# A searched order of products for attention beside a gated layer: another order, its constants, and an earlier spread of one unit's inverses

## The chip, the core and the metric

The kernel runs on one core of a Trainium2 chip. The core has a matrix engine (TensorE, PE in the profile; its weight loads, which overlap the products, are PEld), VectorE (DVE), ScalarE (ACT), GpSimd (POOL) and a queue engine (SyncE, SP), which issues all the DMAs here. Each engine runs its own instructions in the order in which they were written and waits at semaphores for the others. The metric is the device time of one execution in microseconds (us).

## The reference

With x of 2048 rows and 512 columns, float32:

```python
q = (x @ wq).reshape(B, S, H, Dh).transpose(0, 2, 1, 3)      # 32 heads of 16
k, v = x @ wk, x @ wv                                        # one key and value head for all
p = softmax(einsum("bhqd,bkd->bhqk", q, k) * Dh ** -0.5)
a = einsum("bhqk,bkd->bhqd", p, v) ... @ wo                  # heads back to rows, 512 x 512
b = (sigmoid(x @ w_gate) * (x @ w_up)) @ w_down              # 1792 wide
g = sigmoid((x * gate_w).sum(-1, keepdims=True))
out = g * a + (1 - g) * b
```

## The kernel before, in words

The 2048 rows are cut into four blocks of 512. A *unit* is four heads of one block: 32 units (NU), numbered by block and then by group of heads. A unit has four kinds of work.

- *Maximum* (`maximum`, L1141 and L1143): PE multiplies queries with keys, and VectorE reduces each bank of 128 x 512 scores to maxima, which are sent through memory into two spare rows of the queries (`send_max`, `place_max`).
- *Scores* (`scores`, L1150 and L1152): PE multiplies keys with queries, now less the maximum, and ScalarE takes the exponential out of the bank.
- *Values* (`pv`, L1008): PE multiplies the exponentials with the values and a column of ones, in float32, for one of 16 chunks of keys. One call leaves eight matrix records in the trace. Runs of chunks are summed in a bank; at the end of a run ScalarE copies the bank out (`finish`, L1015) and POOL adds it to the unit's sum (`add_sums`, L1022).
- *Division*: the sum is stored (`store`, sd and od), its denominators are loaded in another shape (`sums`, rc), VectorE inverts them (`invert`, L1045), they are stored (`send_inverse`, rd, L1049), loaded back spread over the rows of a head (`spread`, bc, L1055), and POOL multiplies and splits the result into a high and a low part (`divide`, L1063, then L755 and L756: tile o). Two units share one o. The last unit but one (30, NU - 2) has an o of its own: its `spread` issues two loads of bc and two of vd (L1055, L1057), and its `divide` follows alone. Unit 31 is finished at the very end by other code.

Beside this run the projections (`keys`, `query`, `turn`: early, letter G) and the *filling* products (`fill`, L1115): gate, up and down of the second layer, and the output projection of the attention. Jobs of kind "a" project a block's units with wo; for the last block, two jobs "a" do all but the last of four parts, two jobs "e" project unit 30 (they read o), and unit 31's part comes at the end (L1196).

PE's rows are used in two halves of 64. A *pair step* issues one product in each half, of maximum, scores or filling. A filling job fills two banks and changes them over between its halves: when a half has done its first part, an empty instruction on SP (`nc.sync.nop()`, L1119, made in `fill`) waits for that product, and the other half's second part waits for it. The empty instruction stands in SP's own order among the DMAs.

The order of PE is a string, ORDER. V is one chunk of values, G a projection, a dot a pause of the planner's clock of 25 units that issues nothing, and any other letter a hexadecimal digit: its two parts, over 4 and modulo 4, are what each half does (1 maximum, 2 scores, 3 filling, 0 nothing). Before the kernel is written out, `plan()` walks through the string with a clock of its own, in units of a hundredth of a pair step. For each step it puts down the work that follows (banks to reduce, copies, sums, DMAs) at the place at which, by its constants, that work may begin; these places set the orders of the other engines. LATE, RED, EXP, COPY and so on are those constants; FREE and FREE_A are what passes until a bank is free again; IN and OUT are the changes between V or G and pair steps, VALUES one chunk. `event` handles the chain of the division, `may` and `run` the tasks of POOL, and `issue_f` reckons when a turn-over is seen.

In the planner's division chain each link is put down at the first step after its due time. `store` adds 470 to SP's clock and is due to land before `sums`; then come `invert`, `send_inverse`, `spread` and `divide`:

```python
elif what == "send_inverse":
    self.after(self.send(1, 8) + SAFE, "spread", *args)
elif what == "spread":
    u = args[0]
    at = self.issue(250, 128)
    if u % 2 or u == NU - 2:
        self.task(2, at + 2 * SAFE, "divide", u)
```

`send` and `issue` give the time at which the planner takes the data to have landed. No link of the chain changes its own instruction by being put down elsewhere; on the chip each instruction still waits for the data that it reads.

Of the kernel before, what the change touches and what calls it, by code (L numbers as in the profile page):

```python
# [26 lines left out]
NU = NB * NG  # L27
# [10 lines left out]

LATE, LATE_A, FREE, FREE_A = 190, 200, 65, 60


RED, GATED, SUM, ENDS, INVERSE, LOWER = 260, 258, 285, 115, 70, 285

MAX_SPLIT, SQUARE, SEND_SQUARE, PLACE = 180, 75, 220, 320
EXP, COPY, SCALED = 208, 210, 247
TAIL, TAIL_A = 38, 52

SEEN = 10  # L50


IN, OUT, VALUES = 52, 106, 371

CAST, TWO, CAST_W, TWO_W = 265, 556, 450, 1030

# [1 line left out]
ISSUE, SMALL, TEN_KB, LAST, SAFE, SURE = 185, 750, 20, 300, 300, 150  # L58
# [64 lines left out]
class State:  # L123
# [170 lines left out]
    def event(self, what, args):  # L294
        self.acts.append((what, *args))
        if what == "load_x":
            self.x_loaded[args[0]] = self.send(KC, 1024)
        elif what == "store_q":
            at = self.send(2, 512)
            self.q_ready[tuple(args)] = at  # L300
            self.ba_release(("query", *args), at)
        elif what == "send_max":
            self.after(self.issue(SEND_SQUARE, 16) + SAFE, "place_max", *args)
        elif what == "max_square":
            self.after(self.on("dve", self.now, SQUARE) + TAIL, "send_max", *args)
# [360 lines left out]


ORDER = (
    "GGGGGGG555G55G555G55........5GG55G555GG555GG77777Gffdfdffffddddddfffffffff7775.5..GG555GG555G55G9efef7ee7edf6f9f"
    "fb777b7bfefedeedfbd9fbfb75VVV5edeeedff6f9fbb7ef7b7b7bbdfdebfd9fb7bffddd5VV566VVVV977b7bbff9f6fef6defedeedef7ede7"  # L670
    "fbf9bf6bffb5VV555VVVdedef97bf6f6fee7fbdb7b7bbfddefb7edb7ff7ddd5VVVV7b7bb7fedbdbdbe7fedededeef7b7fb7be7dbffddd5VV"
    "VVV67bbb77ffedaf7dbfededeeddbfb7b7fb7ef6efdfd5VV665VVVV7b7bb7bfdedbbd7efedededee7f7bf9fbf67bfedef5VVVVV7b7b7bb7f"
    "bdbdedefedededeef7b7fb7edb7bffddd5VV659VV97b77bbffedaf77efededeede7fb7fef6f9e7fbdbf5VVV555VVV7b7bb7fbdedbdedbfe7"
    "eededef7e7f9f6fedbff7b79V659VV566VVdedeb7f9fe7bdef9e7fb7bb77fbbdbfe6fdfbdfddd5VVV566VV56aV97fefbdbdbf6fb7bfdeded"
    "ee7fb7b7edbe7fedff755VVVVVdededeedef7be7b7fb7b7bb7bfdedfbde7bf9fbdef5VV656VV959VV7b7b79fbfbde7edbfededeede7fb7f6"
    "f9fee7b7ffd9V659VV656VVVded6effb79fef9f6fe7b7bb7bdfdbfbdbf9e7fedef5VVVVV7b9bb77ff9feed7bedfededeef77bbf7b7eded7f"
    "7ddVVVV6b7fedf9f6fbdee7fedb7b7b7ef9fdef6fbedfbdb7dVVV659VV6a5V7b7bbdfededeedb7f6fafbV595VVV7b7bbdfededeed7bfe7bb"
    "dVV9b7b7f7ef6febdfbfdedededbfb76fee7e7f9fe77dbVVVVVVdedeedede7f6fb7bbf7b7b7bbdff9fb7eeded7bffd5VV655VVVdede6fe7f"
    "b7ef9f6f9fb7b7bbdfedfe7edbf9fb7fdaVVVVV7b7bb7b7bfdedebdfedededeef7e77bfbdb7bfedef5VV655VVV7b97b7bffbdbdef9fedede"
    "dedbfb7ef76fef6fb7ef5V9a6VV665VV959VV6dedefe7fedb7bb7defb7bb7bfdbdfedb7be7effee6V959VV956VV956VV7b7afddbf9f6fbed"  # L680
    "fb7ededeef7b7f9f6fbf6fedf75VV59aV692aVV569VV56effedefbdaf7f6bfdb7b7bbdfdbbfd6fef7f7ddd5VVVV7b7bdbedfe7ef6dbfb7ed"
    "ededbf7bb7f6fedebfdfb5VVVVV7b7b79bffbdafdf6fededeedef7e7fb7e7eedff7b5bV95aVVVVV977bfbdef9fb7e7ebdfedeedef7b77bf9"
    "fef6f9ff5eV595VVVVV7b7b7bbdf9fafde7edfedeede7ff6ef7edb7bfefb7aV995VVV565VV7b7b7bbdfeedfedb7fededee7ef7edef97efb7"
    "bbd7bVVV599VVV7b7bb77bbdfbededfedededeef77eef7edbb7fefb75VVVV9edff6edf6fef97bdbfb7b7bbfd6fdefedef7df7775VVV959VV"
    "97b7fbdefbdeb7f9f6fededeef7b7f9faf7b7deff5dVVVVV7b7edbdbf6f9fb7bfededeedef7e7f6f6fef9fb7fb9VVVV969VV6b7bfde7fed6"
    "fede7efbb77bbdfedfedbdb7eeffb75VV596VV596VV997ffbf6f9fbb7dbefdededee7f6ff6f9f7efbff79aVV955VVVV7b7b7b9ff9fbe7edf"
    "edededee7ff6fb76fedefbfb76VV5a9VVVde5eefb7f9fee7dbfbf7ba77fedfedef9bf7bdff755VVVVVdeded6effb7bf9f6fe7b7bb7bfd9ff"
    "ed6fbdeff75dbVVVV65aV6deedffb7b7b7bdbffdde5VV696Vdede6fbf7b7b7bdefbdfd6VVV9b7fde7bfbdbdbb7fedededeef76ffb7bfa7fd"
    "ff5d5VVVVV7b5bbffedb7ee7bdf6fededeedf7bf6faf7f9fff7aaVVV995VVVdee6fdf6fe7bb7fedfb7b7bbdfbd9fef9f6fe7ffd56VVVV6ed"
    "ededff6fb7be7fbdb7b7bbfdedfb79febdf6fef5VV665VV995VV6deedf7bfb7eedf6fbdb77bb7efdeedfedbf9bf7fb5V695VV956VV95aVV6"  # L690
    "7bff9dbf6fef6eddefb7bb7bdfbd7bf6fedefbfedaV695VV695VVVV7b7b7bf9fbdef6.dbdefedeedef7b7ef6fdef6ff7b5a..7V599VV5aaV"
    "V96aVV6eddfef6f6f9fe7bbfdb77bb7efedfed9fbf9b7fdf5VV569VVVV7b7bb7fededeb7f9fe7edededbf7bfe7bb7edbfdfd5VVVV677bbfd"
    "ef6f9feb7bfdededee7fb7ef79fe7bfffd55VVV659VV7b97bfbfded6fbbdf6feeddee7f7bf6fafdf6fbdf5bVVVVV6deef7dbf6fafd7bedfb"
    "7bb7bfdedf9feb7f6bdfef5VV956VVV97bb7b7ffbdedbe7fededeede7fb7fede7bbdf7f7d5VVVVV97fb7bdefb79fbe7efdededee7fb7dbfe"
    "7bdbf6fefaV955VVVVV6dedefe7f6fb7ebdef7b7bb7bdf9ffbdbde7ebfdfd6V695VVVV7b7b7bbdf9fbedf6fedededee7f7ef6f6febdfb7bf"
    "6V959VVVVV6deedef7fe7bedb7dbfb7bb7bdfedefd6fbdbfff575VVV9a6VV696V6ddeeff9f6f9fe7bfbdb7bb7bdff97bfedb7efedef5VV66"
    "9VV559VVV7b7b7bf9fbdeed7efe7ededeef7b7fedef6f9fb7bf9VV569VV6deeeddffb7bf6deb7fb7bb7bdf9ffe7bdeedff7d57VVVVV977bb"
    "7bffbdbedf9fedeeddee7f6ff6f6fbb7efdf76VVV995VVV5b7b7bfefed9fe7bf9fedededef6ff6fb7bfbdeb77dVVV955VVV7b97fbfededed"
    "efefbb7afdfffe7b7b7bf6fedfe5VVVV6dedefe7fe7bbddbfe7b7bb7bdfbdf6fedbe7bdff5dVV659VVV7b7bb7bdf9febd7efededeede7f7e"
    "bf7bde7bf7fde9VVV5a6VV59aV7b7b7b7bbfdbdeedfedededeef7e7fe7e7bf9fbdf75VVVVVV5eedef7efe79febdfb7b7b7bbfd9fbdfb7bf6"  # L700
    "defeddVV655VVV7b7bb7bdfbde7edbdefededee7fe7fe7b7bbddeff76V9a9VV665VV596VV5bbfdeefde76fbdef9f7bb7bbfddbfb7be7f9ee"
    "fedeV659VV695VV56aVV6ddeef7efedb7ebdb7fb7bb77efedfedbdbb7fedf5bV956VV5aaVV96aVVV97bff9e7f6fbf9f97efededeef7b7f9f"
    "6fb7ff7ddd5VVVV7b7bb77bfedbf9defedededeef7b7fe7b7edeef7bf5VV596VV956VV95effef6fedbedf6fb7b7b7bbfdedfbde7ebdbff7d"
    "5VVVV65aV6ddefbf9fe7ef6f9fbdb7b7bbfd7befdbde7efbdd7dVVVVV67bb7bfdf9fbf6edef7ededeef7b7f9faf7dbfe7efbb777VVVVVV9f"
    "dbbdfbe6fdfedededeef76fbf6fdb7efb7f95VV955VVV7b7b97bffedef6dbf9fededeef77e7bf6fef9bbffd5VVVVV7b7b7bb7fedafdedfbd"
    "ededeef7b7fe7e7ef9f9ff76V595VVVVded6fbf6fede7bf97efb7bb7bdff9fb7edeb7dffdd6VV659VVV5e7bfebdfe7edeb7fedbb7b7bbfdf"
    "f9b7fe7fdeded6VV966VVVV7b7bb7dbf9fbdeffedededee7fe7ef6edfefb7b7b79VV959VVVV7b97fbe7f9fbdee7fe7edeedef7dbfaf9f7ef"
    "7ff759VVV966VV5bb7feedfbde7edefe7b7bb7bdff9defedb7e7fd7f6VVV999VVV7b7bb7fedbdef9f6fe7ededee7ffbde7b7befdbb5fdV59"
# [548 lines left out]
```

## Time and profile before

| what | value |
|---|---|
| median of three runs | 1583.95 us (1583.82 to 1584.93) |
| time of the profiled execution | 1582.52 us |
| its span, first to last instruction | 1580.7 us |
| busy: PE, PEld, DVE, ACT, POOL | 1567.2, 1009.0, 1338.9, 1232.2, 803.8 us |
| granted clock of PE, mean | 0.998 |
| DMA | 103.43 MB, mean 65 GB/s |

The largest groups are the reduction of the maxima on VectorE (2048 times, 1253.7 us busy), the exponentials on ScalarE (2048 times, 1040.2 us), and on PE the products of scores, maxima and values. Busy times of PE overlap: two halves run side by side, so the groups of PE add to more than its span. A matrix record's duration includes the time through the array; the distance from start to start tells the pace. The profiled execution's own time is 1.8 us longer than its span, and 1.4 us shorter than the median of the runs.

### The profile page before, as it was taken

The page shows a single profiled execution, that of the slowest core. Times are in us where ns is not written, and L with a number is a line of the kernel's source. Part 1 is how long each engine was busy: PE and PEld are TensorE (multiplying, and loading weights), DVE is VectorE, ACT ScalarE, POOL GpSimd, SP SyncE. Part 2 cuts the span into 40 slices and gives each one's busy share as a digit, 9 for nine tenths or more (in the row PEclk, how much of TensorE's full clock was granted, in tenths as well). Part 3 has the DMA queues.
Part 4 walks back from the last instruction along what each step waited for, and adds up shares of the span by engine and source line. Part 5 has one row for each costly group of instructions (what it writes and reads, how often), then busy time and mean ns, then how long its engine had stood idle before and what let it go on. Part 6 is the DMA issues. An engine that isn't in the chain of part 4 may idle for free.

```text
span 1580.7 us, 33642 instructions
## 1 busy us (share of the span) xinstructions
PE 1567.2 (99%) x12910; PEld 1009.0 (64%) x12910; DVE 1338.9 (85%) x2277; ACT 1232.2 (78%) x2429; POOL 803.8 (51%) x727
## 2 busy tenths in 40 slices
PE   9999999999999999999999999999999999999997
PEld 7766666666666666666666666667675666656653
DVE  6899899988898888889798888888889888988841
ACT  4277878788788787878788777878878887878895
POOL 4353472655574164367475346275547517357351
PEclk9999999999999999999999999999999999999999
DMA  7421120222122121122122212021213202111011
GB/s 245 169 88 51 35 86 16 66 62 83 43 83 66 36 79 53 35 76 71 45 83 63 64 49 78 18 67 60 77 46 92 65 23 87 46 40 59 18 53 40
DMA packets 63076, 103.43 MB, mean 65 GB/s; under 512 B 24530, under 2 KB 24786, under 8 KB 62916
## 3 DMA queue, kind: packets, MB, share of 16 engines
q1 hardware_dynamic: 62916, 101.29, 20.5%
q8 instruction: 101, 1.65, 0.4%
q14 instruction: 59, 0.48, 0.1%
HBM read 79.51 MB, written 21.75 MB: 64 GB/s over the span
## 4 chain that ended last, share of the span: by engine, by line
PE 96%; DVE 1%; DMA 1%; SPq 1%; ACT 0%; issue 0%; POOL 0%; DVEq 0%; ACTq 0%; POOLq 0%
PE bank L1115 32%; PE bank L1008 29%; PE bank L1141 17%; PE bank L1150 16%; PE bank L853 2%; DVE mx L1143 1%; DMA vd<-od 0%; DMA wqr<-wq 0%; SPq L968 0%; DVE q L948 0%; DMA qs<-qd 0%; ACT x L780 0%; PE bank L1196 0%; DVE x L786 0%; SPq L765 0%
## 5 line engine op out<-in xcount | busy, mean ns | idle before, releaser
L1143 DVE TENSOR_REDUCE mx<-bank 128x1 f32<-128x512 f32 x2048 | 1253.7, 680 | 168.7 <-PE bank L1141 104.0
L1152 ACT ACTIVATE p<-bank 128x512 f32<-128x512 f32 x2048 | 1040.2, 664 | 10.9 <-PE bank L1150 7.7
L1150 PE MATMUL bank<-qs,ks 64*128 64x512 f32 x2048 | 723.7, 399 | 0.0
L1141 PE MATMUL bank<-ks,qs 64*128 64x512 f32 x2048 | 684.2, 404 | 0.5 <-DMA qs<-qd 0.5
L1008 PE MATMUL bank<-p,v_aug 128*32 128x512 f32 x4096 | 480.6, 597 | 0.0
L1141 PEld LDWEIGHTS bank<-ks,qs 64*128 64x128 f32 x2048 | 339.8, 184 | 138.7 <-issue 56.5
L1150 PEld LDWEIGHTS bank<-qs,ks 64*128 64x128 f32 x2048 | 359.6, 184 | 91.3 <-ACT p L1152 27.8
L1015 ACT COPY ou<-bank 128x512 f32<-128x512 f32 x205 | 125.0, 610 | 272.3 <-PE bank L1008 124.1
L1022 POOL TENSOR_TENSOR ou<-ou,ou 128x512 f32<-128x512 f32 x174 | 224.3, 1289 | 170.2 <-ACT ou L1015 167.7
L1115 PE MATMUL bank<-wd,hl 64*128 64x512 f32 x1344 | 272.7, 391 | 0.0
L1115 PE MATMUL bank<-x,wu 64*128 64x512 f32 x1344 | 271.3, 390 | 0.6 <-SPq L1119 0.4
L1008 PEld LDWEIGHTS bank<-p,v_aug 128*32 128x32 f32 x4096 | 113.1, 109 | 248.4 <-issue 220.5
L1115 PE MATMUL bank<-x,wg 64*128 64x512 f32 x1344 | 271.2, 391 | 0.0
L1115 PEld LDWEIGHTS bank<-wd,hl 64*128 64x128 f32 x1344 | 199.8, 184 | 20.6 <-issue 2.5
L1115 PEld LDWEIGHTS bank<-x,wg 64*128 64x128 f32 x1344 | 200.8, 184 | 17.5 <-issue 1.2
L1115 PEld LDWEIGHTS bank<-x,wu 64*128 64x128 f32 x1344 | 201.1, 184 | 17.0 <-issue 2.5
L1094 POOL TENSOR_TENSOR ba<-ba,pa_d 128x512 f32<-128x512 f32 x35 | 44.5, 1283 | 93.2 <-ACT pa_d L1091 93.1
L829 POOL CAST wg<-rg 128x1024 fp32r<-128x1024 f32 x27 | 28.0, 1039 | 123.8 <-PE bank L1115 63.9
L829 POOL CAST wu<-ru 128x1024 fp32r<-128x1024 f32 x27 | 28.1, 1040 | 95.8 <-PE bank L1115 93.2
L756 POOL TENSOR_TENSOR wd<-rd,wd 128x512 fp32r<-128x512 f32 x56 | 72.3, 1292 | 4.5
L756 POOL TENSOR_TENSOR hl<-h,hl 128x512 fp32r<-128x512 f32 x56 | 72.0, 1286 | 4.5
L1115 PE MATMUL bank<-wa,o 64*128 64x512 f32 x360 | 70.4, 391 | 0.0
(80 smaller groups left out, 747.2 us busy)
## 6 DMA issues: line engine op xcount, KB each, us to landing
rg<-wg SPq DMA_DIRECT2D x28, 512.0 KB
ru<-wu SPq DMA_DIRECT2D x28, 512.0 KB
rd<-wd SPq DMA_DIRECT2D x28, 512.0 KB
qs<-qd SPq DMA_DIRECT2D x192, 64.0 KB
qd<-q SPq DMA_DIRECT2D x32, 256.0 KB
od<-ou SPq DMA_DIRECT2D x31, 256.0 KB
xf<-x_in SPq DMA_DIRECT2D x16, 256.0 KB
vd<-od SPq DMA_DIRECT2D x32, 128.0 KB
```

Source lines behind the costliest of these rows:

```text
L756: lo.tensor_tensor(hl[:, 1, :], raw, f32(hl[:, 0, :]), op=ALU.subtract)
L829: nc.gpsimd.tensor_copy(WS[item][:, 0, :], raw)
L853: nc.tensor.matmul(ps, w[:, p, part(kc)], X[b, kc][:, q, :], start=i == 0, stop=i == 3 * KC - 1)
L1008: nc.tensor.matmul(ps[32 * j:32 * j + 32, :], v_aug[:, c, :], PT.pop((u, c, j)), start=start, stop=stop)
L1015: nc.scalar.copy(to, ps)
L1022: nc.gpsimd.tensor_tensor(SUMS[u], SUMS[u], PARTS_OF[u].pop(0), op=ALU.add)
L1094: nc.gpsimd.tensor_tensor(BA[b, t], BA[b, t], PA[b, t].pop(0), op=ALU.add)
L1115: ins = nc.tensor.matmul(banks[i], l, r, start=start, stop=stop)
L1141: nc.tensor.matmul(banks[i], qs_t[u % 3][r, pr, part(qt)], ks[r, kb * 512:(kb + 1) * 512], start=True, stop=True)
L1143: nc.vector.tensor_reduce(MX[u][:, pr, h, qt, kb:kb + 1], banks[i], axis=AX.X, op=ALU.max)
L1150: nc.tensor.matmul(banks[i], ks[r, part(c)], qs_t[u % 3][r, pr, :], start=True, stop=True)
L1152: nc.scalar.activation(p, banks[i], AF.Exp, scale=0.25)
```

## The change

Four things change; the functions that issue instructions stay as they are.

- The string ORDER is another one throughout. Both strings issue the same products: 512 V, 24 G, 2048 maxima, 2048 scores and 4404 filling products, in 4251 pair steps before and 4252 after, with 14 dots before and 19 after, 209 runs of full steps (V or G) before and 208 after.
- Constants of the planner are set anew.
- For unit 30, `spread` is due as soon as SP has issued `send_inverse`, and no longer when its data are taken to have landed.
- For unit 30, `divide` is due 1000 units later after the spread than before.

```diff
-LATE, LATE_A, FREE, FREE_A = 190, 200, 65, 60
+LATE, LATE_A, FREE, FREE_A = 186, 190, 62, 62
...
+SPREAD_TWICE = 1000
-EXP, COPY, SCALED = 208, 210, 247
+EXP, COPY, SCALED = 209, 211, 250
...
-IN, OUT, VALUES = 52, 106, 371
+IN, OUT, VALUES = 52, 109, 373
...
         elif what == "send_inverse":
-            self.after(self.send(1, 8) + SAFE, "spread", *args)
+            at = self.send(1, 8) + SAFE
+            self.after(self.sp if args[0] == NU - 2 else at, "spread", *args)
         elif what == "spread":
             u = args[0]
             at = self.issue(250, 128)
             if u % 2 or u == NU - 2:
-                self.task(2, at + 2 * SAFE, "divide", u)
+                self.task(2, at + 2 * SAFE + (u == NU - 2) * SPREAD_TWICE, "divide", u)
...
 ORDER = (
-    "GGGGGGG555G55G555G55........5GG55G555GG555GG77777Gffdfdffffddddddfffffffff7775.5..GG555GG555G55G9efef7ee7edf6f9f"
+    "GGGGGGG555G55G555G55....5...G55GG555GGG555G5dddGf5fff7ffdf7f77..77fffffffff7ddd5GG555GG555GG7.5bfefefbdbfbdb7fed"
...
-    "VVV67bbb77ffedaf7dbfededeeddbfb7b7fb7ef6efdfd5VV665VVVV7b7bb7bfdedbbd7efedededee7f7bf9fbf67bfedef5VVVVV7b7b7bb7f"
...
-    "6VVVV7b7b7b7bfedeedf6dbfededeedff6fbd6fbe7bffb7aV9aaVV596VV956VVVd6eeffdb7bb7b7fed9ffe9VVV7b7bfedbdeededfefb7bb6"
-    "VVV7b7b7b7bfbdededbfedededee7fb7f6f6fedeefbb77V959VVVVde5eedeffb7b7ef6f9fb7b7bbfdf9fbdb7edbfedfe6V6aaVVaaaVVVaaa"
-    "VVVbbbffffefeafeaVVeffefeeffbbbbaVVaaaVVaaaVVabfffffafafbVVeeeeefffffebbbbVbffafbbVaaaVVeeea8VVVV"
...
+    "59VVVdedeedf6f6faf7dbfb7b7bb7bfddbdbfe7ebfde7afeV969V596VV655VVVdedefb7e7b7b7bfedbefadVV969V9b7b7ffedededef6fbfb"
+    "a7V65aV956VVVdedeeddeedfbb77fbb7b7.7b7bfbdbbdfedee7fbdeebVVVVV677bfbf9fbd6fbdefefde6defbf7bbfbffeffeeaa.VVaaaVVV"
+    "aaaVVVeeeffffebfbbbbbbffffffeee.aVVVaaaVVaaaVVbbbffebfffeeeceeeffffffbbbaVVaaaVVaaaVVabbbVVeeeeff3.a2VVV"
 )
```

More of the change, by code (lines that the diff above doesn't have):

```diff
@@ L668 @@
 ORDER = (
-    "GGGGGGG555G55G555G55........5GG55G555GG555GG77777Gffdfdffffddddddfffffffff7775.5..GG555GG555G55G9efef7ee7edf6f9f"
-    "fb777b7bfefedeedfbd9fbfb75VVV5edeeedff6f9fbb7ef7b7b7bbdfdebfd9fb7bffddd5VV566VVVV977b7bbff9f6fef6defedeedef7ede7"
-    "fbf9bf6bffb5VV555VVVdedef97bf6f6fee7fbdb7b7bbfddefb7edb7ff7ddd5VVVV7b7bb7fedbdbdbe7fedededeef7b7fb7be7dbffddd5VV"
-    "VVV67bbb77ffedaf7dbfededeeddbfb7b7fb7ef6efdfd5VV665VVVV7b7bb7bfdedbbd7efedededee7f7bf9fbf67bfedef5VVVVV7b7b7bb7f"
-    "bdbdedefedededeef7b7fb7edb7bffddd5VV659VV97b77bbffedaf77efededeede7fb7fef6f9e7fbdbf5VVV555VVV7b7bb7fbdedbdedbfe7"
@@ L674 @@
[L674 to L708, printed above, removed]
@@ L709 @@
-    "6VVVV7b7b7b7bfedeedf6dbfededeedff6fbd6fbe7bffb7aV9aaVV596VV956VVVd6eeffdb7bb7b7fed9ffe9VVV7b7bfedbdeededfefb7bb6"
-    "VVV7b7b7b7bfbdededbfedededee7fb7f6f6fedeefbb77V959VVVVde5eedeffb7b7ef6f9fb7b7bbfdf9fbdb7edbfedfe6V6aaVVaaaVVVaaa"
-    "VVVbbbffffefeafeaVVeffefeeffbbbbaVVaaaVVaaaVVabfffffafafbVVeeeeefffffebbbbVbffafbbVaaaVVeeea8VVVV"
+    "GGGGGGG555G55G555G55....5...G55GG555GGG555G5dddGf5fff7ffdf7f77..77fffffffff7ddd5GG555GG555GG7.5bfefefbdbfbdb7fed"
+    "edee7fe7ed6fedbfb7bf775VVVdedededefb7b7bf9f6fb7b7bbdfdbfb7bdef7dfddd5VVV659VV977bbf7ef6fbb7edfedededee7f7b7bf9fe"
@@ new lines @@
+    "7bfeedf5VVV6a6VVVVded9fb7fef6f6fedfb7b7bb7bfd9fbde7ef9fffdd55VVV699V977bbf7ef6fbb7defedededee7ff6fb7ede7ef7f775V"
+    "VVVV9dededeffb7bf97edbfb7b7bbdfbdb7fbde7ffdddd5VVVV7b7b7e7bf6fafdf6edfedeeddffa7fb7f6f9f6fff55VVVVVd6defe7ef6fed"
+    "bbdfb7b7bb7bdfbd7efbfe6fdff5d5VVVV6a5V5b7bbff9f9fe7bdbfedededee7f7ebf79fb7befedf9VV655VVVV67befd7ef9feed7eef7bb7"
+    "b7bdfdbfedbb7fe6dffd5VVVVVdedededefb7eb77efb7b7b7bbdff9fedb7bf6ffded5VV659VVV7b7bb7b7fbdededefe7deeedef7f6f9fbde"
+    "f7ff7755VVVVdedeeddefb76fb7efb77bbb7bfdededfedbdbfb7bf5VV659VVVV7b7bb7bfdedbdedbfbdededee7f7bfb76fe7bffded5VV565"
@@ new lines @@
+    "VVVdededeef7e7eb7bdfb7b7b7bbdfdbfbb7bffededed6VV669V5a6V955VVVdedeedef7b7ee77efb7bb7b7bdfbdf9fbdbdeff57ddVV65aV6"
+    "56VVdededefe76f9feb7fb7b7b7bbdfdbf9fbed7efedaf7VVV5a5VV669V5a6Vd9fef6feb77bb7f9fdfdd5VVV7b7bbfdededeedfb7bef57VV"
+    "6deeedf7f9fee7bdbf7b7b7bbdff9fe79fbfe6fdd7dVVVVV6b7efdf6fed6fbedef7b7b7bbfddeefd6fbdbfb7dd7VVVVV7b7bb7f9fbd9fef6"
+    "fedededee7ff6efde7bf9ff7b79V955VVV65aV95aV5eef7bbdfb79fb7bedfedeeddbf7bb7fb7ef6effed6VV659VVVV6b7b7fdbfbd9fbdbef"
+    "dedeede7fb7fe7eb77edeff75VV95aV5a5VVV7b7bdbdef9f6feb7f9fedededfee7ef7e7b7efbfbb9V696V595VVVV699V97b7bff9fe7ef6db"
@@ new lines @@
+    "7efedeede7ff6defedb7bfb7bd7V969V5aaVV695VVVV7b7b7bbfd9fafdf6fedeeddee7ff6fbdef6f9fb7bfdddddVVVVV6defb7f6fb76ffb7"
+    "bb7bdf6fbdeb7f9fbdefdd6VVVV677bbfdbf9fb7ef6edfedeede7f7eefd6fbf7fd7b75VV995VVV97b7fedbf9fbf6dbfe7ededeef7f6bdf6f"
+    "efe7b7f79VVVVV9deeddfefe7b7bdbfe7b7b7bbfdedef79fbe7efdbf5VV965VVVV97bb7b7ffbdef9f6fededeedef77ef9fe7ebd7bff79V65"
+    "aV956VV959VV977bfe7bf9febdb7fedededeef77ebf79fb7bdefef5VVVVV977b7bbffbdef6f9defeddeee7ff6fb7bdbf6f9ffd5VVVVV7b7b"
+    "7bf9fedbe7f6defededeef7b7fb7bdeedfff575VVVVV97b7fbedfbdbf67ef9fededeef77ebdfe7bdfbf6fb5VV699V659VVV7b7bf9e7fedbf"
@@ new lines @@
+    "9fe5bfedede.e7f6ffb7e7bedfb7df5..6VVV59aVVV5bb7bfdbfe7bdebdf6fededee7ff6fbd6f7deff7bbaVV9aaVVVV6b7fdedefbdef6f6f"
+    "9fb7b7bbdfdbbfdb7ede7efef9VV555VVV7b7b7b7bfed9fbedefdedeeddbf7b7bf6fbf6ffddd5VV655VVV6b7bf7defbde7bdbfe7edeededf"
+    "7bfe76fe7bdbff57VVVVVdedef6fb7b7b7bf9fefadeV9a6VVVdedefe7b7b7b7bfedbdf5dVV6deefd7efe7bf9edfb7b7b7bbdfbdfbdb7eed7"
+    "eff5dVVVVV7b7b7b7bbdfedebdefdededee7ff6fe7b7bf9fedf57VV956VVVde6eedf7fe7ef97bbdfb7bb7bdfedbf7edbedf7ff55VV696VVV"
+    "6dedfbdefe7bf97bfedbbb777eff9feedfb7edefbb9V655VVVVV6b7fdbbdfe7ebdf9fe79fe4..edbfb7e7edbdfef6fb7f99VV956VV569VV5"
@@ new lines @@
+    "befe7f9fb7b7eedfb7eeededf7fedbe7ef79fbfbb5VV9a5V6a5V695VV56aVVdedededee7feb77bfb7b7bb7bdfbdefd9fbb7ffde6dV956VVV"
+    "696VVV6fdeedf6fede7bfbf7b7bb7bdf9fbdbf6fbdedff65dVV566VVVd6defbdbfb7bf6f9fb7deeedef7f6f9f9fbe7fff575VVVVVdede7bf"
+    "e7edbdb7ef9f7b7b7bfbf9f9feed7efe7fd5VVVVde6deef7feb7bdfe7fb7b7bbdedfbd9fe7efb7bdd7eVV6aaVVVVVdededefe7b7bf97ef6f"
+    "bbb77bffdbdbdee7fbdefeb6V955VVV97bb77bffbdedbed7efedeedef7e7f9f6fbf6fff755VVV955VVVdededee7fbf6dbfb7fb7b7bbddef9"
+    "fb7bbde7fafdddVVVV67b7b7bffedb7edbedfededeef77bb7f9fbf6ffded5VV665VVVV6dedfe7efede7b7ebf7b7b7bbdfdebfd9fbf9fe7fd"
@@ new lines @@
+    "5VV665VVVVdedef6fb7edbede7fb7bb77bbdfdbf9fbf97efefeeaVV596VV596VV5edefedbf6fee77bf9fb77bb7bff9edfe7ebdffbed5VV65"
+    "5VVVdedede6ffe7eb7dbfb7b7b7bbfddbfbdb7bdeefde7dV956VVVVV6edef7def6fafd7efb7b7bb7bdff9f9fedbf6f6fef5VV956VVV5edef"
+    "efedb7bf9e7f6fb7bbb7fdfedbf9b7fedffd55VVVVV6dedef7bfe76fedbfe7b7b7bbdfbdbdf9fe7efe79fdVVVVV7b7bf9fededede7bfee77"
+    "7VVVdedeef7b7b7b7bfedbdef5VV9def7edbf6fef6f9fe7b7bb7bfdbdfbd6fbf9fed6fdVV696V699V565VVVd6defb7efbdef6f6f9fb7bb77"
+    "bff9efd9fe7eefff59VVV5a6VVVdede6edffb7ef97efb7b7b7bbdfdbfede7bdefaf7f5V95aVVVV6dfebdf6fe79fef6ef7b7b7bbdff9dbfbd"
@@ new lines @@
+    "bdee7fef5VV655VVVVdedede7bf6fee7bdbf7b7bb7bfdedbfd9fefe7af7f5V969V699V565VVV6deedf7bfb79fbf9bf7edeeddfb7bbf76fbf"
+    "6effedaV6a5V955VVVVV5edeedfbfe7af7f9f6fb7b7bbdfedf9fb7bf6ffded6V699V56aV569VVVV97fef6f9fedef6f6fbdb7b7bbfdf9fede"
+    "7bfe6fdf57VVVV5eedeedffb76fedbfb7b7b7bbdfbdeef5fbfedaff75VVVVVdedededee7f6fb7bfb7b7bb7bfdf9bfd6fbdbffdde6V655VVV"
+    "V966V5eedeedffb7ef6f9fb7b7bb7bfdedfbdbf9b7fed6fdVVV655VVV79fee7dbf6fede7ef9fb7b7bbfdbd7efbdbf6fefed5VV659VVV6dfe"
+    "f9f6f6fedebdfb7b7b7bbdfede7f9fef6dbffb5VVVVVdedeede7fb7ef67ebf7b7bb7bdfedfbdbdbf9f6ffe5VVVVV6deedf7ef9f6fef9fb7b"
@@ new lines @@
+    "7bb7bfdbdbdfb7ef7dfd5edVV656VVV5edefb7efede7bdefb7b7bb7bfdedf6fbdedebf7f75VV9aaVVVV97bbb7fdf6f9fbedfe7edeedef7e7"
+    "bf79fef6efd7bbVVVV9a9VV977bbfbdfe76febdfbdededeef7e77ef9fbb7bffed5VV655VVVV6daff7defede7bdb7efb7b7bbdff9defb7ef9"
+    "fe7fd6V6a5V555VVVVdedeedfb7b7bede7fe7bbb77bffd9fbdeb7feffed65VVVVVdededeedef7e7bb7fb7b7b7bbdfdedefbdef6ff7775VV9"
+    "59VVVdedeedf6f6faf7dbfb7b7bb7bfddbdbfe7ebfde7afeV969V596VV655VVVdedefb7e7b7b7bfedbefadVV969V9b7b7ffedededef6fbfb"
+    "a7V65aV956VVVdedeeddeedfbb77fbb7b7.7b7bfbdbbdfedee7fbdeebVVVVV677bfbf9fbd6fbdefefde6defbf7bbfbffeffeeaa.VVaaaVVV"
@@ L712 @@
+    "aaaVVVeeeffffebfbbbbbbffffffeee.aVVVaaaVVaaaVVbbbffebfffeeceeeffffffbbbaVVaaaVVaaaVVabbbVVeeeeff3.a2VVV"
 )
```

## The prediction

> **What bounds the kernel now.** I read the page first, then the busy time by stretches, the chain of waits at the end, and the issues of the DMA queue there. The page's first line and the chain:
>
> ```profile
> span 1580.7 us, 33642 instructions
> ...
> PE 1567.2 (99%) x12910; PEld 1009.0 (64%) x12910; DVE 1338.9 (85%) x2277; ACT 1232.2 (78%) x2429; POOL 803.8 (51%) x727
> ...
> PE 96%; DVE 1%; DMA 1%; SPq 1%; ACT 0%; issue 0%; POOL 0%; DVEq 0%; ACTq 0%; POOLq 0%
> ```
>
> TensorE (PE) is busy for all but 13.5 us of a span of 1580.7. The stretches say where those 13.5 us are (start:end, length, then busy time of each engine, granted clock, DMA):
>
> ```profile
> 5.00:100.00 95.00, 93.50 (x519) 69.25 (x520) 79.73 (x142) 40.29 (x73) 31.12 (x24) 1.00 0.53 181
> 100.00:1545.00 1445.00, 1444.43 (x12185) 924.91 (x12183) 1248.87 (x2117) 1170.26 (x2315) 764.79 (x691) 1.00 0.19 58
> ```
>
> From 100 to 1545 us PE lacks 0.57 us of work in all; from 5 to 100 us it lacks 1.50 us. So a new order can win nothing in the middle: PE has the same products to do, and only their count, the changes between kinds, and stalls can move the time. The stall worth having is in the last 30 us. The same view there:
>
> ```profile
> 1552.80:1555.90 3.10, 1.50 (x11) 0.34 (x9) 0.75 (x1) 2.43 (x5) 0.21 (x1) 1.00 0.19 69
> 1555.90:1559.30 3.40, 1.49 (x6) 0.77 (x8) 0.00 (x0) 0.00 (x0) 2.94 (x3) 0.50 0.00 0
> 1559.30:1562.70 3.40, 3.40 (x17) 1.43 (x17) 2.16 (x3) 2.06 (x4) 0.00 (x0) 0.50 0.00 0
> ...
> 1569.50:1572.90 3.40, 2.40 (x19) 0.86 (x14) 0.90 (x4) 0.86 (x4) 0.00 (x0) 1.00 0.00 0
> 1572.90:1576.40 3.50, 2.15 (x33) 0.56 (x33) 1.94 (x3) 1.09 (x3) 1.26 (x1) 1.00 0.13 48
> ```
>
> PE runs dry after 1554, and then its clock is granted at 0.50 up to 1562.7. The chain there (start, length, what):
>
> ```profile
> 1549.36 6.18 DMA vd<-od
> ...
> 1555.69 1.27 POOL vd L1063
> ...
> 1557.71 1.28 POOL o L756
> ...
> 1559.04 0.79 PE bank L1115
> 1559.83 0.43 PE bank L1150 x2
> ...
> 1561.53 1.60 PE bank L1008 x8
> 1563.13 0.88 PE bank L1150 x4
> ```
>
> PE waits for o of unit 30, made by POOL's divide of the last unit but one, which waits for the last of four loads. The first step with a product on o starts at 1553.81, and the third of them (it reads the low part) would have stood two pair steps later, at 1554.27; it ran at 1559.04: 4.77 us late. At half clock a step then takes 0.43 us.
>
> **The prices.** From the chain, a value step (8 records) and a pair step:
>
> ```profile
> 1296.60 0.66 PE bank L1141 x2
> ...
> 1307.65 0.55 PE bank L1008
> ```
>
> ```profile
> 1503.56 3.57 PE bank L1008 x32
> ...
> 1531.69 1.85 PE bank L1008 x16
> ...
> 1538.86 0.89 PE bank L1150 x6
> ```
>
> Forty-seven pair steps lie between the first two rows: 11.05 us. Three take 0.89. So a pair costs (11.05 - 0.89) / 44 = 0.231 us, and each stretch of pairs 0.20 more. Two values take 1.85 and four 3.57, so a value costs 0.86 and a run of values 0.13 more; a change of kind and back is 0.33.
>
> **The change, part by part.** *The order.* Counting the letters of both strings: V 512 and 512, G 24 and 24; pair steps 4251 and 4252; runs of full steps 209 and 208 (196 with values in each); dots 14 and 19; steps with one empty half 2 and 4, already in the pair count. That is +0.23 for the pair, -0.33 for the run: -0.1. A dot issues nothing, it moves the planner's clock by 25 units (0.06 us at 0.231 us per 100 units): between 0 and 5 x 0.06 = 0.3; I take 0, since all dots of before lie in stretches that lack next to nothing.
>
> *Early stretch.* Other pair steps stand between the projections. At most the 1.50 us are won; as much may be lost. I take 0 and keep +-1.5 for the range.
>
> *The constants.* They do not change what PE does in which order; they change when the planner believes a bank or a result to be there, so the order was allowed to stand closer to its producers. The path over VectorE (LATE + RED + TAIL + FREE) goes from 553 to 546 units, that over ScalarE (LATE_A + EXP + TAIL_A + FREE_A) from 520 to 513: 7 units or 16 ns less room. Where does PE stand at the limit? The weight loads' waits from 100 to 1500 us (total, times, longest) say it:
>
> ```profile
> PEld bank L1141 <- ACT p L1152: 30.4, 55, 0.8
> PEld bank L1150 <- ACT p L1152: 23.0, 61, 0.8
> ...
> PEld bank L1008 <- ACT p L1152: 8.6, 26, 0.6
> ...
> PEld bank L1008 <- DVE mx L1143: 6.6, 22, 0.4
> PEld bank L1141 <- DVE mx L1143: 5.2, 7, 0.8
> ```
>
> 171 places, most of them ordinary changes of kind. Sixteen ns at each is 2.7 us; nothing at each is 0 (and no gain is to be had, since PE lacks 0.57 us here). I take 0.4, near the lower end, because the middle hides its producers today almost wholly. SCALED may turn some sums made by ScalarE and POOL into sums on VectorE or back; both engines lie beside PE (85% and 78%): nothing, and where a queue is full, it shows as the stalls just priced.
>
> *The spread of unit 30.* The DMA queue (SP) at the end, with the unit before for comparison:
>
> ```profile
> 1503.02 0.31 SPq L1049 DMA_DIRECT2D rd<-rc  x1
> 1504.43 0.56 SPq L1055 DMA_DIRECT2D bc<-rd  x1
> ...
> 1535.95 0.56 SPq L1030 DMA_DIRECT2D sd<-ou  x1
> ...
> 1540.24 0.32 SPq L1049 DMA_DIRECT2D rd<-rc  x1
> 1547.60 0.57 SPq L1055 DMA_DIRECT2D bc<-rd  x1
> ...
> 1549.36 0.51 SPq L1057 DMA_DIRECT2D vd<-od  x1
> ```
>
> ```profile
> SPq L1119 <- PE bank L1115: 13.4, 3, 6.9
> ```
>
> The inverses are stored at 1540.24, and 1.41 us later (as for unit 29) they could be read: 1541.65. The four loads start at 1547.60. The second fence (the DMA queue's own waits from 1530 to 1560) has the reason: line 1119 is the empty instruction by which SP tells one half of PE that the other half's bank is turned over. It stands in SP's order ahead of the spread, and waits for a product that ends at 1547.4 (chain, below). That is 5.95 us lost.
>
> ```profile
> 1547.39 0.05 PE bank L1115
> ...
> 1564.02 1.85 PE bank L1008 x16
> ```
>
> ```profile
> 1553.81 0.49 PE L1150 MATMUL bank<-qs,ks 64*128 64x512 f32 x1
> ```
>
> After the change the four DMAs (two bc, two vd) stand right behind rd. They wait for rd's landing, with nothing of use behind them on SP until the output; on POOL nothing follows the divide before the last addition. SPREAD_TWICE only has the planner place the divide 1000 units (2.3 us) later. So far the wait would vanish. But the order around it is new. In the new tail, from the end F of unit 30's last value (before: 1531.69 + 1.85 = 1533.54), come V aaaVV aaaVV, then 27 pair steps, then VV aaaVV aaaVV a, and the first product with o in the next step. Job by job, 18 filling products a half, both turn-overs of the last job fall on the tenth and the fourteenth of the 27. By the constants, the planner reaches them 3800 and 4200 units after F, and the inverse's store only at about 4900 (store 1207, sums 2996, invert 4796): so in SP's order both empty instructions stand ahead of rd itself. Then rd goes out when the fourteenth step has ended: 0.86 + 2 x 2.75 + 14 x 0.231 + 0.2 = 9.8, and 0.2 for SP (1547.4 to 1547.60): F + 10.0. The loads follow at 11.4. From the first load to the low part of o it took 1559.04 - 1547.60 = 11.44: F + 22.85. It is wanted at 6.36 + 6.43 + 1.85 + 2 x 2.75 + about 0.75 = F + 20.9 for the third product. PE waits 2.0 us, where it waited 4.77.
>
> What the present stall costs in all: the step at which PE waits starts at 1553.81 (the last fence, from the timeline), and the next run of values but one at 1564.02. Between lie ten pairs in two stretches and one value: 2.31 + 0.40 + 0.86 + 0.13 = 3.7 us by the prices. They took 10.2: 6.5 us too long, 4.77 of waiting and 1.7 of half clock. With 2.0 of waiting at full clock, 4.5 us are won. From below: 1.6 us, if the clock still halves for as long and the wait shrinks by only a third; from above: 6.5.
>
> **Sum.** -0.1 (counts) + 0.4 (tighter places) + 0 (start) - 4.5 (tail) = -4.2 us. Against the profiled execution's own 1582.52 us that is 1578.3; that execution was 1.4 us below the median, so against the median 1583.95 I say **1579.8 us**. A change under 0.2% (3.2 us) is about what a measurement here cannot tell from none.
>
> **Does the clock stay?** The rows: after a stretch with PE busy 1.50 of 3.10 us the clock fell to 0.50; after 2.40 of 3.40 it stayed at 1.00. The new wait, in two pieces of 1.1 and 0.9 with products between, leaves some 1.6 to 2.0 of 3.4: in between. I take that it stays, at no cost, with 1.7 us at stake. The Trainium skill (TensorE: Matmul & The Clock Gate, "Why this matters for your kernels") advises to avoid idle gaps of PE above about 3 us, one window of idle bringing the clock back to half. By that the clock would stay here and the sum would be the same; the trace is stricter than the page, since the fall came about 1.6 us after PE's last product had ended.
>
> **The rivals.** 1. The turn-overs come behind rd in SP's order, or the inverse is planned earlier than I count. Then rd leaves at F + 6.7 as before, the loads at 8.1, o is there at 19.5, ahead of 20.9, and the whole 6.5 goes: 1577.8. For it: the inverse itself was ready at 1540.2, 6.7 us after F. Against it: my count has a margin of 700 units. 2. The clock halves in the wait that is left: 1.7 us back, 1581.5. 3. The tighter places cost their full 16 ns: 2.7 instead of 0.4, 1582.1; a worse start ends in the same place. 4. Slower: the same places, at each of which PE's next product is late by much more than the constants give, since a late ScalarE result holds PE, which holds ScalarE. It decides from (4.2 + 3.2 + 0.4) / 171 = 46 ns at each; at 60 ns it is 10.3 us in place of 0.4, 1589.7. Against it: PE lacks 0.57 us in 1400 today. 5. The early spread does nothing because rd itself is held: half of this is in my forecast; wholly (a turn-over some 6 us later) it would give the time of before, 1584.
>
> **How the numbers follow.** Forecast 0.44 (its own range 1578.8 to 1581.2); rival 1 0.18; rival 2 0.12; rival 3 0.12; rival 4 0.08; rival 5 0.06. Faster by over 0.2% means under 1580.8: 0.34 of the forecast and all of rival 1, 0.52. Slower: rival 4, 0.08. The rest, 0.40, is within. The range takes rivals 1 to 3 with half of 5: 1577.2 to 1584.0.
>
> **What would show it.** Right: in SP's issues the four loads 1.4 us behind rd; rd later behind F than 6.7, near 10; PE's wait for POOL o near 2 us; granted clock 1.00 up to the end. Wrong at the tail: no wait for POOL o at all (rival 1), or 0.50 there again (rival 2). Wrong in the middle: PE's busy time from 100 to 1500 us short by more than 1 us, or pair steps dearer than 0.231. The prediction falls if the middle lengthens by 3 us or more.

## The result and the profile after

The changed kernel takes 1580.85 us (median of ten runs, 1578.92 to 1582.53); the kernel before, with as many runs, 1583.88 (1581.76 to 1586.09). The ratio is 0.9979, with a 95% interval of 0.9969 to 0.9988: some 3 us faster (1.9 to 4.9), close to the 0.2% that can just be told from nothing. The forecast was 1579.8. In the changed kernel two lines were added ahead of the code that issues instructions, so what was L1115 is L1117, and so on; in the experiments lines move by one to six.

The page's first lines after:

```profile
span 1579.2 us, 33646 instructions
...
PE 1568.4 (99%) x12910; PEld 1006.8 (64%) x12910; DVE 1343.0 (85%) x2283; ACT 1230.4 (78%) x2429; POOL 803.7 (51%) x727
```

The busy time by stretches, the early part and the middle (columns as in the prediction):

```profile
5.00:100.00 95.00, 94.09 (x509) 71.15 (x510) 77.48 (x138) 39.02 (x71) 30.41 (x24) 1.00 0.52 178
100.00:1500.00 1400.00, 1399.16 (x11791) 893.59 (x11791) 1235.61 (x2093) 1124.84 (x2226) 746.02 (x673) 1.00 0.19 58
```

PE still lacks next to nothing in the middle: 0.84 us of 1400. The difference is at the end. SP's issues there, and the chain:

```profile
1541.71 0.54 SPq L1032 DMA_DIRECT2D sd<-ou  x1
...
1549.02 0.32 SPq L1051 DMA_DIRECT2D rd<-rc  x1
1550.48 0.56 SPq L1057 DMA_DIRECT2D bc<-rd  x1
...
1552.24 0.51 SPq L1059 DMA_DIRECT2D vd<-od  x1
```

```profile
1537.39 2.71 PE bank L1010 x24
...
1548.43 0.22 PE bank L1117
...
1548.91 0.02 SPq L1121
...
1549.02 1.39 DMA rd<-rc
...
1552.24 6.06 DMA vd<-od
...
1560.49 1.28 POOL o L758
...
1561.82 0.49 PE bank L1117
1562.31 1.85 PE bank L1010 x16
```

```profile
1555.40:1558.80 3.40, 3.40 (x34) 1.08 (x26) 0.00 (x0) 3.40 (x8) 0.34 (x1) 1.00 0.17 63
1558.80:1562.20 3.40, 2.32 (x16) 0.78 (x8) 0.00 (x0) 3.40 (x9) 2.82 (x3) 1.00 0.00 0
1562.20:1565.60 3.40, 3.40 (x31) 1.65 (x30) 1.26 (x2) 1.46 (x4) 0.00 (x0) 1.00 0.00 0
```

Unit 30's last value is the second of the three in the first row of the chain; it ends at F = 1537.39 + 1.85 = 1539.24. The loads follow rd by 1.46 us instead of 7.36. But rd itself goes out at F + 9.8, where it went at F + 6.7 before: ahead of it in the chain stands the empty instruction of a turn-over (L1121, 1548.91), which waited for a product that ends at 1548.88. The inverse had been ready since 1545.32:

```profile
1545.07 0.25 DVE L1047 RECIPROCAL rc<-rc 128x16 f32<-128x16 f32 x1 [7.17 <-DMA rc<-sd]
```

PE waits twice for o (its own waits from 1530 to 1570 us), and its clock stays at 1.00:

```profile
PE bank L1117 <- POOL o L758: 0.6, 1, 0.6
...
PE bank L1117 <- POOL o L757: 0.5, 1, 0.5
```

The spans (1580.7 and 1579.2) understate the gain, since the two executions began differently. PE's first projection of queries:

```profile
7.34 2.33 PE L853 MATMUL bank<-x,wkv_s 128*128 128x512 f32 x9
9.51 11.05 PE L853 MATMUL bank<-x,wq 128*128 128x512 f32 x48
```

```profile
7.80 3.77 PE L855 MATMUL bank<-x,wkv_s 128*128 128x512 f32 x9
11.40 11.07 PE L855 MATMUL bank<-x,wq 128*128 128x512 f32 x48
```

The first fence is before, the second after: nine products took 2.33 us in the one and 3.77 in the other, and the queries' projection starts 1.89 us later. That is no part of the change (last section). Without it the spans differ by 1.5 + 1.9 = 3.4 us, where the medians differ by 3.0.

### The profile page after: what moved, and what is told of

Its sections match the earlier page's. It is cut to its first block, busy times and chain, and to the rows that moved or that the text cites. A ratio compares the mean times of both kernels' runs of the same rounds, so it can differ in the third digit from the quotient of the medians.

```text
span 1579.2 us, 33646 instructions
## 1 busy us (share of the span) xinstructions
PE 1568.4 (99%) x12910; PEld 1006.8 (64%) x12910; DVE 1343.0 (85%) x2283; ACT 1230.4 (78%) x2429; POOL 803.7 (51%) x727
## 4 chain that ended last, share of the span: by engine, by line
PE 98%; DMA 1%; DVE 1%; POOL 1%; issue 0%; SPq 0%; ACT 0%; DVEq 0%; POOLq 0%; ACTq 0%
PE bank L1117 33%; PE bank L1010 29%; PE bank L1143 16%; PE bank L1152 16%; PE bank L855 3%; DMA vd<-od 0%; DVE mx L1145 0%; POOL wg L832 0%; PE bank L1198 0%; DMA wkv_raw<-wkv 0%; DVE q L950 0%; POOL wkv_s L758 0%; DMA rd<-rc 0%; POOL vd L1065 0%; POOL o L758 0%
## 5 line engine op out<-in xcount | busy, mean ns | idle before, releaser
L1017 ACT COPY ou<-bank 128x512 f32<-128x512 f32 x211 | 129.6, 614 | 276.4 <-PE bank L1010 113.8
L1024 POOL TENSOR_TENSOR ou<-ou,ou 128x512 f32<-128x512 f32 x180 | 231.9, 1289 | 207.3 <-ACT ou L1017 204.5
L1117 PE MATMUL bank<-wd,hl 64*128 64x512 f32 x1344 | 273.3, 391 | 0.3 <-SPq L1121 0.3
L1117 PE MATMUL bank<-x,wu 64*128 64x512 f32 x1344 | 271.3, 391 | 0.6 <-SPq L1121 0.6
L1117 PE MATMUL bank<-x,wg 64*128 64x512 f32 x1344 | 268.6, 391 | 0.0
L1117 PEld LDWEIGHTS bank<-wd,hl 64*128 64x128 f32 x1344 | 201.0, 184 | 26.4 <-issue 7.5
L1117 PEld LDWEIGHTS bank<-x,wu 64*128 64x128 f32 x1344 | 200.8, 184 | 21.6 <-issue 3.4
L1117 PEld LDWEIGHTS bank<-x,wg 64*128 64x128 f32 x1344 | 197.5, 184 | 24.0 <-issue 3.7
L1096 POOL TENSOR_TENSOR ba<-ba,pa_d 128x512 f32<-128x512 f32 x30 | 38.0, 1280 | 86.7 <-ACT pa_d L1093 86.5
L1117 PE MATMUL bank<-wa,o 64*128 64x512 f32 x360 | 69.5, 391 | 0.0
```

The costliest lines, as they stand in the source:

```text
L1017: nc.scalar.copy(to, ps)
L1024: nc.gpsimd.tensor_tensor(SUMS[u], SUMS[u], PARTS_OF[u].pop(0), op=ALU.add)
L1096: nc.gpsimd.tensor_tensor(BA[b, t], BA[b, t], PA[b, t].pop(0), op=ALU.add)
L1117: ins = nc.tensor.matmul(banks[i], l, r, start=start, stop=stop)
```

## The experiments

**One line alone, in the old order.** The kernel before, with this:

```diff
         elif what == "send_inverse":
-            self.after(self.send(1, 8) + SAFE, "spread", *args)
+            at = self.send(1, 8) + SAFE
+            self.after(self.sp if args[0] == NU - 2 else at, "spread", *args)
```

> The kernel before, its order and constants kept, with the one line that makes unit 30's spread due as soon as rd is issued. Theory (the place on SP's queue decides): the four loads start 1.4 us behind rd instead of 7.4, o is there 5.9 us earlier, PE's wait of 4.77 us for it is gone and the clock does not halve: 6 to 6.5 us faster, 1577.4 to 1577.9, ratio 0.996. Rival (the gain of the change comes from the new order): ratio 1.000, 1583.9.

Measured: 1576.34 us, ratio 0.9957 (0.9943 to 0.997); the kernel before stood at 1583.59 there. SP's issues, and POOL's divide:

```profile
1540.24 0.32 SPq L1050 DMA_DIRECT2D rd<-rc  x1
1541.69 0.57 SPq L1056 DMA_DIRECT2D bc<-rd  x1
...
1543.46 0.51 SPq L1058 DMA_DIRECT2D vd<-od  x1
```

```profile
1551.85 1.29 POOL L757 TENSOR_TENSOR o<-vd,o 128x512 fp32r<-128x512 f32 x1
```

The low part of o is there at 1553.14; the third product with it would have stood at 1554.27 in the kernel before. Nothing waits, the clock stays up, and the span falls from 1580.7 to 1574.4: 6.3 us, as expected. So one line of the change, alone in the old order, is worth more than the whole of it. The rival's ratio of 1.000 falls: this gain needs no new order. Whether the line also makes the gain of the change as it stands is for the next run.

**The old rule in the new order.** The changed kernel without that line:

```diff
-            self.after(self.sp if args[0] == NU - 2 else at, "spread", *args)
+            self.after(at, "spread", *args)
```

> The changed kernel with the old rule for unit 30's spread (due when the inverses are taken to have landed). Theory: in the new order no turn-over is left behind rd, so the loads stand right behind rd either way: time of the changed kernel, 1580.9, ratio to before 0.998; loads 1.4 us behind rd, rd near F + 9.8 again (F: end of unit 30's last value). Rival (the line itself is worth something in the new order): 1582 to 1583, ratio 0.999 or more.

Measured: 1581.07 us, ratio 0.9985 (0.9976 to 0.9994), beside 1580.85 with the line. rd went out at 1547.22 and the loads from 1548.67, as with the line. In the new order the line does nothing: both traces show the same sequence of instructions on SP, VectorE, ScalarE and POOL, and PE follows the same string. So the two profiles are two executions of one program, and what differs between them is not the work of the line. The 3 us of the change as it stands therefore come from the rest of the change, the new order and its constants: with the old rule the loads stand right behind rd all the same, since both turn-overs stand ahead of rd. The profile of this run holds something else, in the chain and in the stretches:

```profile
1547.22 1.39 DMA rd<-rc
...
1550.43 7.55 DMA vd<-od
...
1561.48 0.50 PE bank L1117
```

```profile
1558.80:1562.20 3.40, 1.45 (x9) 0.64 (x13) 0.18 (x1) 2.25 (x5) 2.48 (x3) 1.00 0.00 0
1562.20:1565.60 3.40, 3.40 (x18) 0.89 (x12) 0.57 (x1) 0.00 (x0) 0.00 (x0) 0.52 0.00 0
```

The last load took 7.55 us instead of 6.06, for the same bytes in the same place. PE was busy 1.45 of 3.40 us, and here the clock did fall. The tail from 1500 us on is 6.7 us beyond its plain paces (the paces are given below), against 3.6 in the changed kernel's profile. The new order stands on this edge; in the old one with the line nothing waits there.

**rd ahead of the turn-overs, in the new order.** The changed kernel, with unit 30's sums and inverse due earlier in the planner, so that SP issues rd and the loads before the last job's two empty instructions:

```diff
-            self.after(at, "sums", *args)
+            self.after(self.sp if args[0] == NU - 2 else at, "sums", *args)
         elif what == "sums":
-            self.after(self.issue(430, 136) + 2 * SAFE, "invert", *args)
+            at = self.issue(430, 136) + 2 * SAFE
+            self.after(self.now + 1300 if args[0] == NU - 2 else at, "invert", *args)
```

> The changed kernel with unit 30's sums and inverse due earlier in the planner, so that rd and the four loads stand ahead of the last job's two turn-overs on SP. Theory: rd at F + 6.7, loads at F + 8.1, PE's wait for o (1.7 us after) gone; the turn-overs come about 1 us late and cost PE 0.4 us: 1.3 us faster than the changed kernel, 1579.5, ratio to before 0.9972. Rival (the late turn-overs hold PE as long as o did): no faster than the changed kernel, 1581 or more, with PE waiting for L1122's empty instruction 1.5 us or more.

Measured: 1577.97 us, ratio 0.9969 (0.9958 to 0.998). SP's issues and PE's wait:

```profile
1539.83 0.54 SPq L1033 DMA_DIRECT2D sd<-ou  x1
...
1543.50 0.32 SPq L1052 DMA_DIRECT2D rd<-rc  x1
1544.95 0.56 SPq L1058 DMA_DIRECT2D bc<-rd  x1
```

```profile
PE bank L1118 <- SPq L1122: 0.4, 1, 0.4
```

rd now follows the store of the sums by 3.7 us; in the changed kernel it was 7.3 (1541.71 to 1549.02). No wait for o is left, and the late turn-over costs PE 0.4 us. That is what was expected, and the rival price of 1.5 us for the turn-over falls. The inverse comes no earlier for that:

```profile
1543.22 0.25 DVE L1048 RECIPROCAL rc<-rc 128x16 f32<-128x16 f32 x1 [7.19 <-DMA rc<-sd]
```

With F at 1537.36 here that is F + 5.9, and in the changed kernel it was F + 5.8 (1545.07). So rd alone was held, and by the turn-overs alone.

**The loads one turn-over later, in the old order.**

```diff
-            self.after(self.send(1, 8) + SAFE, "spread", *args)
+            self.after(self.send(1, 8) + SAFE + 900 * (args[0] == NU - 2), "spread", *args)
...
-                self.task(2, at + 2 * SAFE, "divide", u)
+                self.task(2, at + (1 + (u != NU - 2)) * SAFE, "divide", u)
```

> The kernel before with unit 30's loads one turn-over further back on SP's queue (behind both turn-overs of the last job). Theory: the loads start when the second one's product ends, near 1550.1 instead of 1547.6, all that waits for o moves by 2.5 us, with the clock halved there as before: 2.5 us slower, 1586.4, ratio 1.0016. Rival (the wait for o is hidden by something else that is late as well, and its length does not matter): ratio 1.000.

Measured: 1585.78 us, ratio 1.0017 (1.0008 to 1.0026), 2.2 us slower. PE's wait:

```profile
PE bank L1115 <- POOL o L755: 6.1, 1, 6.1
```

In the kernel before:

```profile
PE bank L1115 <- POOL o L755: 3.4, 1, 3.4
```

The wait grew by 2.7 us and the time by 2.2 (1.3 to 4.1): within the interval, the length of the wait goes into the time whole.

**PE kept busy while it waits, in the old order.** Thirteen products on the tile of values (v_aug, complete long before), whose result nobody reads, ahead of the first product that uses o:

```diff
+        if alone and j.i == 0 and at == 0 and h == 1:
+            self.acts.append(("warm", self.free.index(min(self.free))))
...
+    def warm(i):
+        for _ in range(13):
+            nc.tensor.matmul(banks[i][:, :P], v_aug[:, :4, :], v_aug[:, 4:8, :], start=True, stop=True)
...
```

> The kernel before with 13 products of 128 columns on constants (3.0 us by the 0.23 us that each takes at the start of the kernel), whose result nobody reads, written into a free bank just ahead of the first product that uses unit 30's o: PE computes while it waits, the length of the wait stays. Theory (half clock is a term of its own, 1.7 us beside 4.77 us of waiting): the granted clock stays 1.00 through the tail, the steps after the wait take 0.23 us and not 0.43, 1.7 us faster than before, 1582, ratio 0.999. Rival (the slow steps after the wait are late data and not the clock): the steps stay at 0.43 us, ratio 1.000.

Measured: 1581.08 us, ratio 0.9982 (0.9973 to 0.9991), with the kernel before at 1583.77. Stretches and chain:

```profile
1556.00:1559.30 3.30, 3.30 (x27) 2.98 (x26) 0.00 (x0) 1.24 (x3) 1.44 (x2) 1.00 0.07 28
1559.30:1562.70 3.40, 2.39 (x18) 1.31 (x21) 1.02 (x2) 0.99 (x3) 1.71 (x2) 1.00 0.00 0
```

```profile
1561.14 0.50 PE bank L1117
1561.64 0.23 PE bank L1156 x2
...
1564.44 1.85 PE bank L1010 x16
```

The clock stays and the steps take 0.23 us, so they were slow by the clock and not by late data. The stretch from the waiting step (1555.81 in the trace) to this run of values takes 8.6 us instead of 10.2: 1.6 us for the half clock, against 1.7 in the sum. The median's 2.7 us has that within its interval (1.4 to 4.3).

**Room on VectorE's path.** What is left between the two orders is the middle. The kernels rd_first and spread_alone have neither wait nor half clock at the end and began alike (9.44 and 9.37 us); their spans are 1576.0 and 1574.4. Of these 1.6 us, 0.4 is the late turn-over. To see whether the rest is the room that the constants took from VectorE's path, both got shorter reductions:

```diff
-        nc.vector.tensor_reduce(MX[u][:, pr, h, qt, kb:kb + 1], banks[i], axis=AX.X, op=ALU.max)
+        nc.vector.tensor_reduce(MX[u][:, pr, h, qt, kb:kb + 1], banks[i][:, :498], axis=AX.X, op=ALU.max)
```

> rd_first with each of the 2048 reductions on VectorE over 498 of 512 scores (14 scores of each bank are left out of the maximum): every bank is given back some 16 ns earlier, the 7 units by which the new constants had shortened that path. The middle's excess over the plain paces from 100 to 1500 us was 34.2 us there and 32.8 with the old order. Theory (the 1.4 us are the room that the constants took away on VectorE's path): about 1 us comes back, excess near 33.2. Rival (the 1.4 us lie elsewhere: ScalarE's path, turn-overs, the order itself): excess stays at 34 within 0.3.

> spread_alone (old order) with the same shorter reductions, 14 scores of each bank left out. Theory (the old order had room there): the middle's excess stays at 32.8 within 0.3. Rival (every tight place gains, old ones too): it falls by as much as with the new order.

The excess named there is worked out from the starts of PE's products, taken along ORDER: the time between neighbouring steps from 100 to 1500 us, less a plain pace for each: 0.229 us for two pairs, 0.872 for two values, 0.330 into values and 0.972 out of them. Measured, with the new order: 34.1 us, 34.2 with whole reductions; with the old one 32.6, 32.8 with whole ones. A reduction took 668 ns instead of 681:

```profile
L1146 DVE TENSOR_REDUCE mx<-bank 128x1 f32<-128x498 f32 x1934 | 1166.7, 668 | 172.7 <-PE bank L1144 96.5 <-PE bank L1153 53.0 <-PE bank L1118 17.1
```

The theory falls, on one profile of each: nothing came back in the middle, so the 1.4 us are not VectorE's room. (The times, 1578.61 with a ratio of 0.9967 and 1575.62 with 0.995, differ from those with whole reductions by less than their intervals.)

What remains is spread thinly. PE lacks 0.37 us of work from 100 to 1500 in spread_alone, and 0.87 in rd_first:

```profile
100.00:1500.00 1400.00, 1399.63 (x11811) 904.17 (x11809) 1229.43 (x2084) 1127.68 (x2229) 741.18 (x668) 1.00 0.19 58
```

```profile
100.00:1500.00 1400.00, 1399.13 (x11794) 894.46 (x11793) 1235.57 (x2094) 1125.02 (x2227) 744.92 (x671) 1.00 0.19 58
```

and the five kinds of place of the prediction, 171 before, are 207 in the changed kernel:

```profile
PEld bank L1143 <- ACT p L1154: 37.6, 70, 0.8
PEld bank L1152 <- ACT p L1154: 24.4, 71, 0.8
...
PEld bank L1010 <- DVE mx L1145: 11.6, 38, 0.4
PEld bank L1143 <- DVE mx L1145: 7.2, 11, 0.8
...
PEld bank L1010 <- ACT p L1154: 5.3, 17, 0.4
```

So about 0.5 us is PE without work. Another 0.3 is no stall: from 100 to 1500 us there are 183 runs of values in the new order and 180 in the old, and the first pair step behind a run takes 0.11 us more than a plain one; both strings have 196 such runs in all. The last 0.6 may be ScalarE's path, or other neighbours among the steps with slightly other paces; no run tells these apart, and none has the old string with the new constants or the reverse. It stays open.

## Why the prediction was right, point by point

*Counts.* Taken at -0.1 us. No run measures so little; nothing speaks against it.

*The early stretch.* Taken at 0. From 5 to 100 us PE lacked 1.50 us before and lacks 0.91 after, but at the slower start that the after profile had; in the two profiles of the new order that began like the one before it lacks 1.34 and 1.80. The four profiles of the old and new order that began alike (before and spread_alone, landed_rule_new_order and rd_first) have their first value at 94.1, 93.9, 93.2 and 93.1 us. Ahead of it stand 127 letters that issue something in the old string and 125 in the new, and 13 and 12 runs of projections; two steps and one run less are 0.8 us at the prediction's prices (0.231 and 0.33), and the starts differ by 0.8 to 1.0. Nothing to be told from 0.

*The tighter places.* Taken at 0.4 us near the lower end of 0 to 2.7, measured 1.4 (rd_first beside spread_alone; excess 34.5 in the changed kernel, 34.2 in its two variants; 32.5, 32.8 and 33.2 in the kernel before, spread_alone and spread_later). This is the term that was mis-sized. The reason for the low choice, that the middle hid its producers before, says nothing about another order; and the mechanism that the term was built on, less room on the two paths, is refuted for VectorE's and open for ScalarE's.

*The spread.* The times held one by one, but not the part of the change that they were put down to. The prediction counted the tail's gain under the earlier spread; landed_rule_new_order has the same times without it (1581.07 beside 1580.85), so the gain is the new order's. The prediction's own finding, both turn-overs ahead of rd, leaves the line nothing to do. Turn-overs stand ahead of rd in the new order; rd at F + 10.0 forecast, 9.8 measured; loads at F + 11.4, measured 11.2; low part of o at F + 22.85, measured 22.5 (1560.49 + 1.28); PE's wait 2.0, measured 1.7 (0.63 and 1.10 beyond the plain pace of a step). The tail beyond plain paces from 1500 us on fell from 8.3 to 3.6 us: 4.7, against 4.5. One count was off: the last line of the new string, as it is quoted under "The change", has one e too many. In the kernel it reads ffebfffeeceee, the stretch between the values has 26 letters and not 27, and the second turn-over falls on the thirteenth. That makes rd and the moment at which o is wanted earlier by some 0.2 us alike, so that the wait came out right all the same.

*The clock.* It stayed, with PE busy 2.32 of 3.40 us. It fell in landed_rule_new_order at 1.45 of 3.40, so rival 2 is the same program with a slower load: that it stayed in the changed kernel's profile is partly luck, and how often it falls over many executions is not known. The price of 1.7 was measured at 1.6.

*The sum.* -0.1 + 1.4 + 0 - 4.7 = -3.4, as the two spans without their different starts; the medians give 3.0. That the sum meets the spans so closely is partly chance: in these two profiles alone the middle differs by 1.9 (34.48 against 32.54), and the stretch up to the first value makes up for it. The forecast's 4.2 lies within the interval of 1.9 to 4.9: right in the tail, and too high by what the middle cost.

*The rivals.* Rival 1 (turn-overs behind rd) is not what the change does, but it is what rd_first makes of it, and there the wait goes as that rival said, for 0.4 us at the turn-over, which the rival had left out. Rival 4 (slower) did not occur. Rival 5 has a true half: the early spread does nothing in the new order, because rd is held; but the time of before does not come back, since the turn-overs are over by F + 9.7. What the prediction did not weigh is that the moved spread in the *old* order is free of every wait: it took the new order as given, and with it the turn-overs that hold rd.

## What to carry to other kernels

An instruction that only waits still holds every DMA behind it on its queue (the loads for 5.95 us in the kernel before, rd for 3.7 in the new order): look at what stands between two DMAs of a chain, and not at the DMAs alone. When a change has several parts, price each one in the old surroundings too; here one line gives 7 us in the old order and nothing in the new, and the whole change gives 3, partly because the new order holds rd, the store for which those loads wait. A planner's clock is a guide to order, not to time: by its constants rd leaves 4900 units or 11 us after F, where rd_first shows that it can leave at 6.1 (F there 1537.36, rd 1543.50), and so it let the turn-overs go first.

## What the runs showed of the hardware

PE does not start at the same pace in every execution of the same program. By the start of the queries' projection the nine profiles fall into two groups: 9.36 to 9.51 us in five (before, spread_alone, landed_rule_new_order, rd_first, old_order_room) and 11.06 to 11.42 in four (after, spread_later, kept_busy, new_order_room). The changed kernel and landed_rule_new_order, one program, are in different groups. In the later ones the nine products ahead of it take 3.4 to 3.8 us instead of 2.3. The traces' record of the granted clock begins, at 1.00, at 4.5 to 6.3 us in the five and at 10.2 to 11.0 in the four. The start costs 1.6 to 2 us, more than half of what the change moved, and it may be a good part of the 3 to 4 us between the fastest and the slowest run of a kernel. The Trainium skill (TensorE: Matmul & The Clock Gate, "What's actually happening") says that the window by which the clock is set runs freely and does not begin with the kernel. These traces agree, by the same 4.5 to 6.3 and 10.2 to 11.0 us.

Late in the kernel the clock fell behind stretches in which PE was busy 1.45 of 3.40 us (landed_rule_new_order, with gaps of 1.9 and 0.6 us) or 1.50 of 3.10 (before), and stayed behind 2.32 and 2.39 of 3.40 (changed kernel and kept_busy). A threshold on the busy time does not follow from this, for at the very end of kept_busy the clock stayed behind 1.54 of 3.42:

```profile
1573.94:1577.36 3.42, 1.54 (x32) 0.31 (x16) 2.16 (x3) 0.70 (x2) 1.26 (x1) 1.00 0.22 81
1577.36:1580.77 3.41, 0.00 (x0) 0.00 (x0) 0.00 (x0) 0.00 (x0) 0.00 (x0) 1.00 0.62 231
```

What decides between these cases no run here tells.
